# A gated linear recurrence and a token/channel mixer in one kernel: fp32 prefix sums in batch 0, upper halves read in place, and a written-out order

## The chip, the cores and the metric

The kernel runs on one core of one Trainium2 chip. The metric is the device time of one execution in microseconds, smaller is better. PE is the tensor engine, DVE the vector engine, ACT the scalar engine, POOL the GpSimd engine, SP the engine whose queue issues most transfers.

## The reference

All inputs are fp32. Per batch (4) and head (8) a state of 48 x 48 is decayed and updated over 768 steps; its output, laid out as 768 x 384 per batch, goes through a mixer.

```python
f = 1.0 / (1.0 + np.exp(-f_logit))
for t in range(S):
    state = f[:, :, t, :, None] * state + np.einsum('bhd,bhe->bhde', k[:, :, t], v[:, :, t])
    y[:, :, t] = np.einsum('bhd,bhde->bhe', q[:, :, t], state)
x = y.transpose(0, 2, 1, 3).reshape(B, S, H * D)
h = np.maximum(x.transpose(0, 2, 1) @ w_tok1, 0.0) @ w_tok2      # 768 -> 256 -> 768
u = x + h.transpose(0, 2, 1)
out = u + np.maximum(u @ w_ch1, 0.0) @ w_ch2                     # 384 -> 1536 -> 384
```

## The kernel before

The recurrence is done in chunks. A group (b,d) is batch b and one third d of the sequence, 256 steps on 128 partitions, two steps in each. For a group the kernel does this, by the names of its operations:

- four loads of 384 KB on SP's queue (`ldf`, `ldq`, `ldk`, `ldv`, L412), each into one of a few tiles per input;
- `exp` and `ln` on ACT (L536, L538) turn f_logit into Ln = log(1 + exp(-f)), the negative log of the gate; `P` on DVE (L543) adds the two steps of a partition into Pf;
- `hi` (ACT or POOL) casts Pf to bf16 in Phi, `lo` (L548) puts the rest Pf - Phi in Plo; `cums` on PE multiplies both with a triangular matrix (L556, L557: the prefix sums) and with two column masks (L561, L562: the totals), so that bf16 matmuls give nearly fp32 sums;
- `S0` on DVE (L566) subtracts Ln from the sums, which gives those of the even step; `gl`, `G`, `Gi` on ACT (L574, L577, L579) are the exponentials of the totals, of the negative sums and of the sums;
- `qh`, `kh` (L607, L618) are q and k times these factors, in bf16; they are transposed, on PE in batches 0 and 1 (L641) and by a transposing transfer in batches 2 and 3 (L653); `ev` copies them out of PSUM;
- `sc` on PE (L769, L725) are scores, `mk` on DVE (L776, L733) masks them into AmT, `av` (L786, L740) multiplies with v in bf16 (`U`, v_bf); `ds` (L672, L662) is the state's increment, `s`, `t`, `M`, `bm`, `bs` carry the state, `qm`, `qn` (L798, L749) add its share to y; `xev` (L823) copies y to xu, and `xb` casts it to x_bf.

After the three groups of a batch comes its mixer: `tok1` (L839), Relu `h1` (L844), `tok2` (L855), the add `u` (L861), a cast to u_bf, transposes `uP` (L876) and their copy `uT`, then `ch1` (L902) with Relu `z` on ACT or DVE (L909, L911), `ch2` (L927), the add `o` (L937) and the stores (L946), two per pair of row tiles, all on SP's queue.

w_tok1 and w_tok2 are loaded as fp32 by SP after batch 0's loads and cast on chip; w_ch1 and w_ch2 are loaded by POOL's queue, which converts them to bf16, in two halves each, behind a copy (`gate_`, L435) that waits for an earlier load.

No engine's order is written by hand. Each operation is given to a `Planner` with the engines that may do it, a cost for each, its inputs and outputs, and a priority `prio`, by default a due time from `due`, `at` and `at_gate`. `Planner.run` (L87) walks through planned time: of all ready operations it takes the one that can start first, and among equals the one with the smallest `prio`. It also chooses the tile from each pool and the PSUM bank (8 banks; `P.spare` keeps bank 7 out of use until planned time 26). The program is then issued in planned order, and each engine works through its queue strictly in that order, whatever the real times are. Where PE's plan has a gap before planned time 60, matmuls on a constant tile `idle` (L983, called fillers here) are put in, so that PE doesn't stand still.

Of the kernel before, what the change touches and what calls it, by code (L numbers as in the profile page):

```python
# [8 lines left out]
FP32 = mybir.dt.float32  # L9
# [3 lines left out]

SEM = 0.06
PE_LAT = 0.10
SW_LEAD, HW_LEAD = 3.9, 3.7


def act_t(n):
    return (0.05 + 0.835e-3 * n, 0.12)  # L20

# [8 lines left out]

def pe_mode(name):

    if name.startswith("sc"):
        return "s"
    if name.startswith("ds"):
        return "d"
    return "v" if name.startswith("av0") else "n"
# [7 lines left out]
class Planner:  # L45


    def __init__(self):
        self.ops, self.by_name = [], {}
        self.pools, self.group_pool, self.group_of = {}, {}, {}  # L50
        self.producers, self.touch = {}, {}
        self.bank_pools, self.banks, self.quota, self.warm = {}, [], None, 0.0
        self.held, self.spare, self.slack, self.patience = [], 0.0, {}, 0.0
# [33 lines left out]
    def run(self):  # L87
# [31 lines left out]
        while ready:  # L119
            best = None  # L120
            cache = {size: self._banks(size) for size in (1, 2)}
            for o in ready:
# [23 lines left out]
                for e, (occ, lat) in o.eng.items():  # L146
# [6 lines left out]
                    key = (round(st + self.patience * max(o.prio, -20.0), 2), o.prio, st + occ)  # L153
# [17 lines left out]
            if o.xfer is not None and e == "POOL":  # L171
# [12 lines left out]
                end = sw + 0.3  # L184
# [49 lines left out]
    @staticmethod  # L234
    def switch(a, b):
        if a == b:
            return 0.0
        return (0.095 if a == "s" else 0.0) + (0.093 if b != "n" and a != "s" else 0.0)
# [22 lines left out]
def kernel(  # L261
# [23 lines left out]
    XB_FROM = 2  # L285
    DEEP = 2
# [28 lines left out]
    Pf_tiles = [st([128, H, D], FP32, f"Pf{i}") for i in range(2)]  # L315
    P.pool("Pf", Pf_tiles)
    L_tiles = [(st([128, H, 64], BF16, f"Phi{i}"), st([128, H, 64], BF16, f"Plo{i}")) for i in range(2)]
    P.pool("L", L_tiles)
    P.pool("U", [st([128, 2, DM], BF16, f"v_bf{i}") for i in range(3)])
# [27 lines left out]
    P.patience = 0.0  # L347
    P.spare = 26.0
# [29 lines left out]
    def consts():  # L378
# [4 lines left out]
        for hi, lo in L_tiles:  # L383
            nc.vector.memset(hi[:, :, D:64], 0.0)
            nc.vector.memset(lo[:, :, D:64], 0.0)
        nc.vector.memset(halves, 0.0)
# [6 lines left out]
        nc.vector.tensor_scalar(tri2[0:64, 0:64], tri[0:64, 0:64], -1.0, None, ALU.add)  # L393
        for r in (slice(0, 64), slice(64, 128)):
# [13 lines left out]
    def load(nm, b, d, prio, after=()):  # L408
# [4 lines left out]
             prio, after, xfer=ROW * 128 * H)  # L413

    for b in range(B):
        seq = [(nm, c + 1 if nm == "f" else c) for c in range(-1, NP) for nm in "fqkv"]
        if b == 0:
            seq = [(w[0], int(w[1])) for w in "f0 f1 q0 k0 f2 v0 q1 k1 v1 q2 k2 v2".split()]
# [8 lines left out]
    gates = dict(zip(("wc1a", "wc1b", "wc2a", "wc2b"), ("w2s1", "-", "q1,1", "-")))  # L427
    sw = []

    def sw_dma(nm, outs, fn, n, mb):  # L430
# [6 lines left out]
        P.op(nm, {"POOL": (0.7 * n, 0)}, [], outs, fn, -899.5 + len(sw), dep, xfer=mb / 0.31)  # L437
        sw.append(nm)
    w1s = st([128, 3, 2, DT], FP32, "w1s")

    def flat(v):
        return P[v].rearrange("p h two d -> p (h two d)")
    tail = f"~ldv0,{NP - 1}"
    for n in range(2):
        P.value(f"w2s{n}", f"w2s{n}", "vk"[n])
    P.op("w1l", {"SP": (0.7, 0)}, [], ["w1s"], lambda: nc.sync.dma_start(
        out=w1s.rearrange("p g two c -> p g (two c)"),
        in_=moe_w_tok1.rearrange("(g p two) c -> p g (two c)", p=128, two=2)), -400, [tail], xfer=0.786 / 0.35)
    tail = "~w1l"
    for j in range(2):  # L450
        for kk in range(2):
            P.op(f"w1c{j},{kk}", {"POOL": pool_t(768), "ACT": act_t(768)}, ["w1s"], [f"w1{kk}"],
                 lambda e, j=j, kk=kk: cast(
                     e, w_tok1[64 * j:64 * j + 64].rearrange("p (g kk) c -> p kk g c", kk=2)[:, kk],
                     w1s[64 * kk:64 * kk + 64, :, j]), T0 - LEAD - 4 + kk)
    for kt in range(2):
        P.op(f"w2l{kt}", {"SP": (0.7, 0)}, [], [f"w2s{kt}"],
             lambda kt=kt: nc.sync.dma_start(out=flat(f"w2s{kt}"), in_=moe_w_tok2[128 * kt:128 * kt + 128]),
             -390 + kt, [tail], xfer=0.393 / 0.35)
        tail = f"~w2l{kt}"  # L460
        for th in range(2):
            P.op(f"w2{kt},{th}", {"ACT": act_t(384), "DVE": dve_t(384)}, [f"w2s{kt}"], [f"w2{th}"],
                 lambda e, kt=kt, th=th: cast(
                     e, w_tok2[:, kt, 384 * th:384 * th + 384].rearrange("r (c two p) -> r c two p", two=2, p=64),
                     flat(f"w2s{kt}")[:, 384 * th:384 * th + 384].rearrange(
                         "r (c p two) -> r c two p", p=64, two=2)), T0 - LEAD - 2 + th)
    P.by_name["ldf1,0"].after = (tail,)
    for hf in range(2):
        cols = slice(hf * (DCH // 2), (hf + 1) * (DCH // 2))
        sw_dma("wc1" + "ab"[hf], ["wc1" + "ab"[hf]], lambda cols=cols: nc.gpsimd.dma_start(  # L470
            out=w_ch1[:, :, cols], in_=moe_w_ch1.rearrange("(kt p) n -> p kt n", p=128)[:, :, cols]), 1, 1.18)
    for hf in range(2):
        kts = slice(hf * (NCC // 2), (hf + 1) * (NCC // 2))
        sw_dma("wc2" + "ab"[hf], ["wc2" + "ab"[hf]], lambda kts=kts: nc.gpsimd.dma_start(
            out=w_ch2[:, kts], in_=moe_w_ch2.rearrange("(kt p) n -> p kt n", p=128)[:, kts]), 1, 1.18)

    def cast(e, o, x):
        if e == "ACT":
            nc.scalar.copy(o, x)  # L479
        else:  # L480
            (nc.vector if e == "DVE" else nc.gpsimd).tensor_copy(o, x)  # L481
# [11 lines left out]
    def attention(b, d):  # L493
# [21 lines left out]
        P.value(f"Ln{i}", f"fld{i}", "f")  # L515
# [15 lines left out]
        def qkT(z, e):  # L531
# [3 lines left out]
        P.op(f"exp{i}", {"ACT": act_t(768)}, [f"f{i}"], [f"E{i}"],  # L535
             lambda: nc.scalar.activation(f_(), f_(), AF.Exp, bias=0.0, scale=-1.0), pg - 6)  # L536
        P.op(f"ln{i}", {"ACT": act_t(768)}, [f"E{i}"], [f"Ln{i}"],
             lambda: nc.scalar.activation(f_(), f_(), AF.Ln, bias=1.0, scale=1.0), pg - 5.5)  # L538
        flex = {"POOL": pool_t(384, True), "DVE": dve_t(384)} if b == 0 else {"POOL": pool_t(384, True)}

        def vec(e):
            return nc.vector if e == "DVE" else nc.gpsimd
        P.op(f"P{i}", {"DVE": dve_t(384)}, [f"Ln{i}"], [f"Pf{i}"], lambda: nc.vector.tensor_tensor(  # L543
            P[f"Pf{i}"][:, :, 0:D], f_()[:, :, 0], f_()[:, :, 1], ALU.add), pg - 5, port=True)
        P.op(f"hi{i}", {"POOL": pool_t(384), "ACT": act_t(384)}, [f"Pf{i}"], [f"hi{i}"],
             lambda e: cast(e, P[f"L{i}"][0][:, :, 0:D], P[f"Pf{i}"][:, :, 0:D]), pg - 4.5)
        P.op(f"lo{i}", flex, [f"hi{i}", f"Pf{i}"], [f"L{i}"],
             lambda e: vec(e).tensor_tensor(  # L548
                 P[f"L{i}"][1][:, :, 0:D], P[f"Pf{i}"][:, :, 0:D], P[f"L{i}"][0][:, :, 0:D], ALU.subtract), pg - 4,
             port=True)  # L550

        def cums():
            o = P[f"S1{i}"][:, 1]
            hi, lo = P[f"L{i}"]
# [9 lines left out]
        P.op(f"cums{i}", {"PE": (0.54, PE_LAT)}, [f"L{i}", f"hi{i}"], [f"S1{i}"], cums, pg - 3.5 + pe,  # L564
             after=[] if g2 < 0 or gi_sb else [f"~av{b2},1", f"~ds{b2}"])
        P.op(f"S0{i}", {"DVE": dve_t(384)}, [f"S1{i}", f"Ln{i}"], [f"S{i}"], lambda: nc.vector.tensor_tensor(  # L566
# [5 lines left out]
        def gi_out():  # L572
            return f_().rearrange("t h j d -> t j h d") if gi_sb else sv()
        P.op(f"gl{i}", {"ACT": (0.12, 0.12)}, [f"S1{i}"], [f"gl{i}"], lambda: nc.scalar.activation(  # L574
# [6 lines left out]
            after=[f"G{i}", f"gl{i}"] + ([f"S0{i}", f"P{i}"] if gi_sb else []))  # L581
# [12 lines left out]
        else:  # L594
            P.op(f"U{i}", {"POOL": pool_t(768), "ACT": act_t(768)} if b == 0 else {"POOL": pool_t(768)}, [f"v{i}"],
# [34 lines left out]
        if not xbar:  # L630
            for j in range(2):
                T = f"T{i},{j}"
                for nm in "qk":
# [8 lines left out]
                    P.op(f"tr{nm}{i},{j}", {"PE": (0.25, PE_LAT)}, [f"{nm}h{i},{j}"], [f"{T}{nm}"], tr,  # L642
# [7 lines left out]
        else:  # L650
            for e in range(2):
# [3 lines left out]
                         P[f"qh{i}"][64 * e:64 * e + 64]), pr - 500, xfer=1.3)  # L655
# [35 lines left out]
        if whole:  # L691
            P.op(f"bs{i}", {"ACT": (0.55, 0.12), "POOL": (0.6, 0.1)}, [f"s{i}"], [f"bs{i}"], lambda e: bs(e), pr + 2.05)
        else:
            P.op(f"bs{i}", {"ACT": (0.55, 0.12)}, [f"dS{i}"], [f"bs{i}"], bs, pr + 1.5, excl=f"dS{i}")
# [326 lines left out]
```

## Time and profile before

| | us |
|---|---|
| median of 4 runs (lowest, highest) | 184.63 (184.15, 185.4) |
| profiled execution, own time | 184.15 |
| its span, first to last instruction | 182.4 |
| PE, DVE, ACT, POOL busy | 169.6, 121.2, 119.3, 67.7 |
| first ch1 matmul / last ch2 matmul starts | 40.3 / 177.6 |

The span is from the first to the last instruction; the own time has about 1.75 us around it. Matmuls are pipelined: a row's duration of 326 ns for 384 columns is latency, and the next one starts about 162 ns later. The granted clock was 0.997.

### The profile page before, as it was taken

The numbers are of one execution on the slowest core, as the hardware profiler recorded it, in microseconds if no ns is written. First come the engines' busy times: TensorE is split into PE (matmuls) and PEld (weight loads), VectorE is DVE, ScalarE is ACT, GpSimd is POOL, SyncE is SP. The second block draws the span as 40 slices with busy tenths as digits, with TensorE's granted clock in tenths as the row PEclk, the third lists the DMA queues.
The fourth block names the chain that finished last, engine by engine and source line by source line (L and its number), as shares of the span: only waits on it lengthen the run. The fifth ranks groups of instructions, "written<-read, shape, count | busy, mean of one in ns | idle before, by whom it ended". The sixth has DMA issues, their size and how long they took to land.

```text
span 182.4 us, 5036 instructions
## 1 busy us (share of the span) xinstructions
PE 169.6 (93%) x2044; PEld 105.4 (58%) x2050; DVE 121.2 (66%) x232; ACT 119.3 (65%) x215; POOL 67.7 (37%) x114
## 2 busy tenths in 40 slices
PE   6999969999999999999989999789999999999990
PEld 2346646576566766565656666366666666666650
DVE  7479875698767687998499996998935166012021
ACT  2879689999676688767777935469238442924800
POOL 3017783466373347386543936265110100000000
PEclk9999999999999999999999999999999999999998
DMA  6999999999993999989999999991352021303033
GB/s 150 261 261 263 303 324 223 209 246 259 207 218 79 278 262 262 185 181 208 213 270 201 198 281 175 214 205 17 57 89 59 0 62 28 86 0 88 4 94 79
DMA packets 69159, 31.00 MB, mean 170 GB/s; under 512 B 63120, under 2 KB 68496, under 8 KB 69136
## 3 DMA queue, kind: packets, MB, share of 16 engines
q1 hardware_dynamic: 66768, 28.32, 73.2%
q0 software_dynamic: 2368, 2.36, 7.8%
q8 instruction: 16, 0.26, 0.6%
q14 instruction: 7, 0.06, 0.1%
HBM read 25.17 MB, written 4.72 MB: 164 GB/s over the span
## 4 chain that ended last, share of the span: by engine, by line
PE 63%; DVE 13%; ACT 11%; DMA 6%; issue 3%; DVEq 0%; POOL 0%; ACTq 0%; POOLq 0%
PE pp L902 24%; PE pp L927 22%; DMA v_ld<-in_v_dram 4%; DVE xu L861 3%; DVE qkh L618 3%; PE pp L855 3%; ACT f_ld L538 2%; ACT f_ld L536 2%; DMA f_ld<-in_f_logit_dram 2%; PE pp L839 2%; PE pp L725 2%; ACT xu L823 2%; PE pp L876 1%; PE pp L740 1%; DVE qkh L607 1%
## 5 line engine op out<-in xcount | busy, mean ns | idle before, releaser
L927 PE MATMUL pp<-w_ch,zT 128*128 128x384 bf16 x288 | 52.2, 326 | 0.0
L902 PE MATMUL pp<-uT,w_ch 128*128 128x384 bf16 x288 | 51.5, 326 | 0.6 <-DVE zT L911 0.4
L909 ACT ACTIVATE zT<-pp 128x384 bf16<-128x384 f32 x72 | 34.9, 490 | 18.1 <-PE pp L902 17.9
L902 PEld LDWEIGHTS <-w_ch 128*128 128x128 bf16 x288 | 26.9, 98 | 17.2 <-issue 1.0
L927 PEld LDWEIGHTS <-zT 128*128 128x128 bf16 x288 | 27.0, 98 | 16.5 <-issue 0.2
L937 DVE TENSOR_TENSOR xu<-xu,pp 128x384 f32<-128x384 f32 x24 | 13.2, 551 | 29.2 <-PE pp L927 29.0
L481 POOL CAST v_bf<-v_ld 64x384 bf16<-64x384 f32 (+1 forms) x28 | 16.1, 576 | 16.2 <-DMA v_ld<-in_v_dram 12.7
L983 PE MATMUL pp<-idle 128*128 128x512 bf16 (+5 forms) x76 | 19.7, 346 | 1.7 <-DVE idle L379 1.5
L776 DVE TENSOR_TENSOR AmT<-pp,msk 128x1024 bf16<-128x1024 f32 x12 | 14.4, 1219 | 3.1 <-PE pp L769 3.1
L911 DVE TENSOR_SCALAR zT<-pp 128x384 bf16<-128x384 f32 x24 | 12.7, 554 | 4.6 <-PE pp L902 3.7
L733 DVE TENSOR_TENSOR AmT<-pp,msk 128x1024 bf16<-128x1024 f32 x12 | 14.1, 1217 | 2.4 <-PE pp L725 2.3
L481 POOL CAST x_bf<-xu 128x768 bf16<-128x768 f32 x10 | 8.2, 822 | 20.0 <-ACT xu L823 20.0
L607 POOL TENSOR_TENSOR qkh<-q_ld,G 128x384 bf16<-128x384 f32 x14 | 13.0, 940 | 2.4 <-ACT glast L574 2.3
L618 DVE TENSOR_TENSOR qkh<-k_ld,pp 64x384 bf16<-64x384 f32 x24 | 13.2, 550 | 0.5
L983 PEld LDWEIGHTS <-idle 128*128 128x128 bf16 x82 | 8.0, 106 | 8.6 <-issue 3.6
L861 DVE TENSOR_TENSOR xu<-xu,pp 128x384 f32<-128x384 f32 x24 | 11.7, 546 | 0.2 <-PE pp L855 0.2
L536 ACT ACTIVATE f_ld<-f_ld 128x768 f32<-128x768 f32 x12 | 10.1, 839 | 2.6 <-DMA f_ld<-in_f_logit_dram 2.5
L548 POOL TENSOR_TENSOR Plo<-Pf,Phi 128x384 bf16<-128x384 f32 x10 | 9.1, 912 | 7.1 <-ACT Phi L479 3.2
L823 ACT COPY xu<-pp 128x768 f32<-128x768 f32 x11 | 8.8, 797 | 4.4 <-PE pp L786 2.3
L577 ACT ACTIVATE G<-pp 128x768 bf16<-128x768 f32 x12 | 9.7, 812 | 2.7 <-DVE pp L566 2.6
L855 PE MATMUL pp<-h1T,w_tok 128*128 128x384 bf16 x48 | 9.9, 325 | 1.0 <-DVE xu L937 0.6
L479 ACT CAST u_bf<-xu 128x768 bf16<-128x768 f32 x8 | 6.5, 831 | 6.4 <-DVE xu L861 6.2
(99 smaller groups left out, 246.7 us busy)
## 6 DMA issues: line engine op xcount, KB each, us to landing
f_ld<-in_f_logit_dram SPq DMA_DIRECT2D x12, 384.0 KB, 5.0
q_ld<-in_q_dram SPq DMA_DIRECT2D x12, 384.0 KB, 6.0
k_ld<-in_k_dram SPq DMA_DIRECT2D x12, 384.0 KB, 5.9
v_ld<-in_v_dram SPq DMA_DIRECT2D x12, 384.0 KB, 6.4
out_dram<-xu SPq DMA_DIRECT2D x22, 192.0 KB, 2.8
w_ch<-in_moe_w_ch_dram POOLq DMA_DIRECT2D x4, 576.0 KB, 9.3
w1s<-in_moe_w_tok_dram SPq DMA_DIRECT2D x1, 768.0 KB, 7.6
v_ld<-in_moe_w_tok_dram SPq DMA_DIRECT2D x1, 384.0 KB, 6.1
```

The lines of the kernel that those rows point to most:

```text
L481: (nc.vector if e == "DVE" else nc.gpsimd).tensor_copy(o, x)
L536: lambda: nc.scalar.activation(f_(), f_(), AF.Exp, bias=0.0, scale=-1.0), pg - 6)
L607: vec(e).tensor_tensor(o, x, g, ALU.mult)
L618: nc.vector.tensor_tensor(o, x, g, ALU.mult)
L733: lambda e=e: nc.vector.tensor_tensor(P[f"Am{e}{i}"], P[f"A{e}{i}"].rearrange("p b (a t) -> p (b a) t", t=128), msk2.rearrange("p j t -> p ...
L776: lambda j=j: nc.vector.tensor_tensor(P[f"Am{j}{i}"], P[f"A{j}{i}"].rearrange("p b (a t) -> p (b a) t", t=128), msk[:, j].rearrange("p j t ...
L855: nc.tensor.matmul(pm[:, 0:DM], lhsT=w_tok2[:, kt, tt * 128:(tt + 1) * 128], rhs=P[f"h1{b}"][:, kt, :], start=(kt == 0), stop=(kt == 1))
L861: nc.vector.tensor_tensor(x, x, P[f"up{i}"][:, 0:DM], ALU.add)
L902: nc.tensor.matmul(pm, lhsT=w_ch1[:, kt, cc * 128:(cc + 1) * 128], rhs=uT[:, 3 * th:3 * th + 3, kt, :], start=(kt == 0), stop=(kt == 2))
L909: nc.scalar.activation(P[f"z{i}"], P[f"zp{i}"][:, 0:384], AF.Relu)
L927: nc.tensor.matmul(P[f"op{i}"][:, 0:DM], lhsT=P[f"z{b},{th},{cc}"][:, c0:c0 + 128], rhs=w_ch2[:, cc, :], start=(cc == 0), stop=(cc == NCC ...
L983: nc.tensor.matmul(P.psum_tile[:, bank, 0:n], lhsT=idle[:, 0:128], rhs=idle[:, 0:n], start=True, stop=True)
```

## The change

1. `HIV`: the upper half of Pf is no longer cast into Phi. `hi_of` views the fp32 tile Pf as bf16 and takes every second element, so it is cut off, not rounded; `lo` is Pf minus that view. This holds in every group that still uses bf16 sums.
2. `F32P`: in batch 0, groups (0,1) and (0,2), the sums are fp32 matmuls on Pf itself: `mln` (minus Ln by a negative identity), `cums` (both halves of S at once) and `cumt` (the totals). `lo` and `S0` fall away there.
3. The order: `RANKS`, a table of 967 numbers, replaces the priority of every operation. Costs in the planner are changed a little, and bank 7 is kept out of use until planned time 30.
4. The last row tile of batch 3: ch2 and its add are done in two halves of 192 columns, and the stores of the last two tiles go to two queues, SP's and ACT's.
5. Loading and casting of w_tok1 and w_tok2 stay (`WSW = 0`, `COLS = 0`); the code for another way is not used.

The changed kernel's lines have other numbers: ch1 L1042, ch2 L1090 (last tile L1080), tok1 L973, tok2 L995, uP L1016, cums L650 and L651, fp32 sums L673, L679, L685, fillers L1153, stores L1109.

```diff
+RANKS = """
+560 561 562 563 564 565 566 567 568 569 570 571 573 574 575 576 577 578 579 580 581 582 583 584 587 588 589 590 591
...
+901 906 905 907 494 694 627 754 489 615 488
+"""
...
-                    key = (round(st + self.patience * max(o.prio, -20.0), 2), o.prio, st + occ)
+                    key = (int(st * 100.0 + 0.5), o.prio, st + occ)
...
+    HIV = 1
+    F32P = 2
+    F32 = 0
+    WSW = 0
...
-    Pf_tiles = [st([128, H, D], FP32, f"Pf{i}") for i in range(2)]
+    Pf_tiles = [st([128, H, 64 if HIV else D], FP32, f"Pf{i}") for i in range(2)]
...
-    P.spare = 26.0
+    P.spare = 30.0
...
+        f32p = F32P and b == 0 and d >= F32P - 1
...
+        def hi_of():
+            if HIV:
+                return P[f"Pf{i}"].bitcast(BF16).rearrange("p h (d two) -> p h d two", two=2)[:, :, :, 1]
+            return P[f"L{i}"][0]
...
+        def minus_ln():
+            nc.tensor.matmul(hd(P[f"S{i}"][:, 0, 0:DM]), lhsT=tri2f[:, 1], rhs=f_()[:, :, 1], start=True, stop=False,
+                             skip_group_check=True)
+
+        def cums32p():
+            x = P[f"Pf{i}"]
+            for a in (1, 0):
+                nc.tensor.matmul(hd(P[f"S{i}"][:, a, 0:DM]), lhsT=tri2f[:, 0], rhs=x[:, :, 0:D], start=(a == 1),
+                                 stop=(a == 0), skip_group_check=True)
+
+        def totals32p():
+            o, x = P[f"S{i}"][:, 1], blk(P[f"Pf{i}"])
+            for hp in range(HP):
+                nc.tensor.matmul(o[:, DM + 2 * hp:DM + 2 * hp + 2], lhsT=x[:, hp], rhs=halvesf, start=False,
+                                 stop=(hp == HP - 1), skip_group_check=True)
...
+            if b == B - 1 and tt == NCH - 1:
+                for n in range(2):
+                    c = slice(n * (DM // 2), (n + 1) * (DM // 2))
...
+                    def oadd(i=i, s=s, c=c, n=n):
+                        x = P[f"o{i}"][:, s, c]
+                        nc.vector.tensor_tensor(x, x, P[f"op{i},{n},0"][:, c], ALU.add)
...
+                if single:
+                    for j, (q_, e) in enumerate(((nc.sync, "SP"), (nc.scalar, "ACT"))):
+                        P.op(f"out{b},{tts[0]},{j}", {e: (0.6, 0)}, [f"o{b},{tts[0]}"], [],
+                             lambda store=store, j=j, q_=q_: store(js=(j,), eng=q_), due(b, "o", tts[-1]) - 500, xfer=0.45)
+                    continue
...
+    for o, rank in zip(P.ops, RANKS.split()):
+        o.prio = int(rank)
     total = P.run()
```

## The prediction

> **What bounds the kernel now.** I read the page's busy shares first, then the chain of waits, then the windows, then the groups by form.
>
> ```profile
> PE 169.6 (93%) x2044; PEld 105.4 (58%) x2050; DVE 121.2 (66%) x232; ACT 119.3 (65%) x215; POOL 67.7 (37%) x114
> ...
> DMA  6999999999993999989999999991352021303033
> ```
>
> PE looks full, but 82 of its matmuls are fillers (L983), and "busy" is pipelined time. So I price PE by start-to-start spacing. The chain of waits gives it: 36 matmuls of 384 columns in 5.85 us, 162.5 ns each; four 128-column transposes in 0.22; 32 scores in 0.57; 8 of L740 in 0.20; 4 of L749 in 0.17.
>
> ```profile
> 15.03 6.96 DMA v_ld<-in_v_dram
> 22.02 0.81 ACT v_bf L479
> ...
> 30.91 0.43 ACT w_tok L479
> 31.33 0.74 ACT f_ld L538
> 32.08 0.74 ACT xu L479 x2
> ...
> 35.77 2.66 DVE xu L861 x6
> ...
> 40.39 1.06 PE pp L902 x6
> ...
> 171.91 5.86 PE pp L927 x36
> 177.79 0.55 DVE xu L937
> ```
>
> Counting matmuls at these spacings, PE had 16.6 us of work before the first ch1 (L902, 40.3) and stood idle or on fillers for 23.7. From there to the last matmul (178.1) it had 128.2 us of work and lost 9.6: 1.9 in 40 to 60, 1.2 in 60 to 80, 2.1 in 80 to 112, **2.9 in 112 to 123** (batch 2's passage from tok1 to ch1), 1.5 after. So the time is the start, plus 128.2 of PE work, plus 9.6 of holes, plus a tail of 4.3. The start is no longer transfers alone: v of (0,2) lands at 22.0, but the last x_bf ends at 33.1, behind masks on DVE and weight casts on ACT.
>
> ```profile
> 20.00:30.00 10.00, 7.84 (x204) 5.66 (x206) 7.69 (x11) 7.50 (x11) 8.11 (x13) 1.00 1.05 304
> 30.00:40.00 10.00, 9.54 (x125) 6.44 (x125) 7.35 (x16) 9.94 (x18) 4.89 (x6) 1.00 1.08 216
> ```
>
> The columns that matter are the third and fourth engine, DVE and ACT: each has slack in the first stretch, and ACT none in the second.
>
> **What the Trainium skill says.** "FP8 and Floating Point Precision", TensorE Precision Notes: true FP32 is four passes through the array. No row of before shows it. Estimate from that page and our spacing: 4 x 160 ns = 0.64 us for 384 columns. "TensorE: Matmul & The Clock Gate", the section on 56 against 53.3 ns, gives N / 2.4 GHz + 2.5 ns and a floor of about 25 ns; the trace agrees (162.5 ns at 384, 25 ns for the 2-column L561). "SBUF — State Buffer", Door 1, says bf16 may be strided by up to 8 elements for free within 16-byte lines; the new upper halves step by 2, so they would cost nothing. No run here shows it yet.
>
> **The change part by part.**
>
> ```profile
> L479 ACT CAST Phi<-Pf 128x384 bf16<-128x384 f32 x8 | 4.1, 510 | 4.1 <-DVE Pf L543 4.0
> L481 POOL CAST Phi<-Pf 128x384 bf16<-128x384 f32 x4 | 2.3, 566 | 11.0 <-DVE Pf L543 11.0
> L548 POOL TENSOR_TENSOR Plo<-Pf,Phi 128x384 bf16<-128x384 f32 x10 | 9.1, 912 | 7.1 <-ACT Phi L479 3.2 <-issue 2.1 <-PE pp L855 1.5
> L556 PE MATMUL pp<-Phi,tri 128*128 128x384 bf16 x12 | 3.9, 325 | 0.0
> ```
>
> *Upper halves as a view.* All 12 Phi casts go: 4.1 us of ACT, 2.3 of POOL, and one hop per group. After batch 0 neither engine is the bound, so I cost that at nothing. In group (0,0) Plo follows Pf directly: 7.45 becomes 6.9, worth 0.5 at the first G. If strided reading ran at half speed, L556 and the four L561 would add 0.16 + 0.10 per group, 10 groups, 2.6 us; a gain in reading there cannot be. I take 0.
>
> *fp32 sums for (0,1), (0,2).* Out go a Plo (0.56 on DVE or 0.91 on POOL), an L566 (0.56 DVE) and a bf16 sum of about 0.53 on PE, twice. In come three fp32 matmuls of 384 (3 x 0.64 = 1.9) and four of 2 columns; for these I take 0.1 each (0.03 to 0.3), since four weight passes must be slower than one. That is 2.3 against 0.53 on PE, covered by fillers at 8 to 10.4. For (0,2) it is partly bare: score (0,1) and eight transposes of (0,1) stand behind it on PE; I put that score at 17.2, against 19.2 now. DVE loses 1.7 us and gains 0.45 of constants, which end before its first wait (6.3). Bounds for the start: -1 to +2.
>
> *Order table.* Every operation gets a rank; engines and tile slots are chosen again. I walked the new queues with the durations of the groups (back to back, DVE starts a 384-column operation every 0.47, masks every 1.12, ACT a 768-column one every 0.74). ACT without casts: exp and ln of (0,1) end at 7.9, G0 starts 9.0 (10.4 before), Gi0 ends 10.7. DVE: gates of (0,0) to 11.8, copies to 13.1 (both on DVE now), mask (0,0) 15.4, kh (0,1) to 17.5, mask (0,1) 17.8, masks of (0,2) from 24.6 to 26.9 instead of 28.2 to 30.5, one w_tok cast, the last x_bf at **28.5 instead of 33.1**. ACT keeps pace: w1s lands at 24.0, the w_tok2 halves at 25.0 and 26.3 as now, x copies at 27.4 to 28.3, f of (1,0) lands at 28.0. Then tok1 29.2, two Relus with an ln between 30.7, tok2, six adds and two Pf to 34.6, u_bf on POOL 35.0, transposes, uT 36.1: ch1 at **36.1 to 38; I take 37.0**, the upper part for waits that I do not see (the trace has 0.2 to 1.1 us of "issue" on PE). Queues passed: SP's first 15 loads keep their order; q and k of (0,2) now reuse the first tiles, free at 10.9 and 11.8, their issue 11.8 and 13.5, no wait. f of (1,1) must now wait on SP for kh (0,2) at 22 (it was issued at 20.5), with q, k and v of (1,0) behind it, but the transfers themselves are behind until 28. On POOL three w1s casts and an x_bf stand ahead of the w_ch1 issue: 27.7 instead of 27.07, landing 7.9 later as now, 35.6, and the second half 38.5 plus 0.7. So the weights nearly bind. The 16 transposes of (1,0) (0.9 us) move behind ch1. **Net of the start: -3.3 + 0.9 = -2.4** (-4 to +1).
>
> After that: (1) in 40 to 112 the holes were 5.2. ACT takes most Relus, no DVE pair of masks stands ahead of the first z; but batch 0's ch2 are used up before batch 1's passage, where six adds, four kh, a ch2 add and a state product precede one uT. DVE has 11 us there and PE 12, by the spacings above. I take 0 (-2 to +3). (2) Batch 2's passage: tok2 follows tok1 bare (Relu 0.5 + 0.2), then two adds less before the first two u_bf. Add 0.55, cast 0.83, transposes 0.33, copy 0.80 after the fourth tok2, less scores, transposes, sums in between: 1.9 of hole, was 2.9: **-1.0**. (3) Batch 3: all 18 transposes come together with one ch2 behind them, copy 0.80 less 0.49: **+0.5**.
>
> *Spare bank* until 30 instead of 26: holds a bank for fillers; I cost it inside the walk, since only planned order depends on it. *Weights*: same loads and casts, only other engines.
>
> *Tail.*
>
> ```profile
> 174.51 4.97 SPq L946 DMA_DIRECT2D out_dram<-xu  x6
> 175.91 0.56 DVE L937 TENSOR_TENSOR xu<-xu,pp 128x384 f32<-128x384 f32 x1 [1.47 <-PE pp L927]
> 177.79 0.55 DVE L937 TENSOR_TENSOR xu<-xu,pp 128x384 f32<-128x384 f32 x1 [1.33 <-PE pp L927]
> ```
>
> The last tile's 12 matmuls become 24 of 192 columns (82.5 ns by the page's formula, 24 x 82.5 = 1.98 against 1.95). The last add shrinks from 0.55 to 0.35 (192-column L697: 344 ns). Its two stores are issued at 178.3 and 178.9 on SP; now one each on SP and ACT, the second 0.5 earlier if ACT's issue is as quick, which no row shows (0 to 0.6 saved). **-0.6.**
>
> Sum: -2.4 - 1.0 + 0.5 - 0.6 = -3.5. From the profiled execution (span 182.4, own time 184.15, 1.75 around) 180.65; the median of four stands 0.48 above it: **181.1, say 181.0**.
>
> **Rivals.**
> *A, weights or unseen waits bind the start* (0.18). If w_ch1 lands some 2 us later, because more loads are queued ahead of it by then, ch1 starts at 39.3: start -0.1, total 183.3. For it: transfers are full to 40. Against: bytes and their order are the same.
> *B, the holes go too* (0.17). Relus move to ACT and ranks were set over all queues at once; if half of 9.6 goes beyond my sum, 181.0 - 3 = 178. Against: DVE keeps 12 + 12 masks at 1.2.
> *C, slower: the passage to ch1 runs bare in all three later batches* (0.18). PE has no ch2 left for filling there: add, cast, transposes, copy are 2.5 us; batch 1 +1.9, batch 2 +1.5 (two masks, 2.3 us, stand among the adds), batch 3 +2.0. Then +5.4 - 3.0 + 0.5 gives 187. It decides once the bare wait is over about 1.7 us per batch. For it: tok2 is followed at once by 18 transposes in batch 1. Against: DVE's own sum there is below PE's.
> *D, strided reading at half speed* (0.02): 2.6 us, 183.7, no change. That the view is not used can be excluded from the queues: no Phi cast is left.
>
> **Numbers.** The main case has 0.45 (179.3 to 183.0). Faster by over 0.5% (below 183.7; 0.5% is about what a measurement of this kernel tells from no change): main 0.45, B 0.17, 0.08 of A: 0.70. Same: 0.10 of A, D: 0.12. Slower: C, 0.18. Range 177.3 to 186.0: it leaves out the far end of B (0.05) and the upper part of C (0.12).
>
> **What would show it.** First ch1 near 37 with last x_bf near 28.5; fp32 matmuls 0.64 apart; L650 still 325 ns with 160 to its successor; PE's hole in batch 2's passage under 2; the last store issued within 0.5 of the last add. Wrong if ch1 starts after 39, if fp32 matmuls take over 1 us, or if PE waits over 1.7 us in each passage.

## The result, and the profile after

Median of the changed kernel: **186.03 us** (43 runs, 184.26 to 188.16); before, beside it, 184.81 us (64 runs). The ratio is 1.0038, 95% interval 1.002 to 1.0057: slightly slower, where 181.0 was forecast and 186.0 was the end of the range. The profiled execution took 184.55 us, its span is 182.8 us. These comparisons leave disturbed runs out.

The page after, busy shares and the clock by slices:

```profile
PE 170.2 (93%) x2046; PEld 107.6 (59%) x2051; DVE 117.5 (64%) x225; ACT 116.7 (64%) x209; POOL 64.9 (35%) x115
...
PEclk9999999999999999999999999999999999999999
```

As the diff says, DVE, ACT and POOL have less to do. But the first ch1 (now L1042) starts at 40.87, not at 37.0, and 0.9 us of transposes have moved behind it. The windows show where the holes went: the changed kernel first, then the one before; the third figure is TensorE's busy time.

```profile
80.00:84.00 4.00, 2.40 (x40) 1.85 (x39) 3.91 (x9) 2.70 (x4) 3.27 (x7) 1.00 0.90 167
...
116.00:124.00 8.00, 6.96 (x88) 4.01 (x87) 7.61 (x13) 4.79 (x9) 3.71 (x9) 1.00 0.99 173
```

```profile
80.00:84.00 4.00, 4.00 (x38) 2.41 (x37) 3.39 (x7) 2.77 (x5) 3.36 (x7) 1.00 1.07 259
...
116.00:124.00 8.00, 6.59 (x112) 4.25 (x112) 7.69 (x14) 4.85 (x9) 2.94 (x6) 1.00 1.09 211
```

Batch 1's passage (around 80) is worse, batch 2's (around 118) a little better. By the prediction's count (a hole is time of TensorE that its work, taken at start-to-start spacings, doesn't fill) the holes after the first ch1 fell by about 0.5 us: +1.5 to +1.9 in batch 1's passage, -0.8 to -0.9 in batch 2's, less than 0.2 either way after 124, and about -1.1 to -1.3 in the stretches between. The span's +0.4 is then the sum of a first ch1 that is 0.55 later, 0.4 more from there to the last matmul (0.9 of work more, 0.5 of holes less) and a tail that is 0.55 shorter.

What stands ahead of the first ch1 is seen best on TensorE's own timeline (start, duration, instruction, idle time before it), changed kernel:

```profile
25.45 0.23 PE L1153 MATMUL pp<-idle 128*128 128x128 bf16 x1
25.60 0.30 PE L903 MATMUL pp<-qkT 48*64 48x128 bf16 x5
27.47 0.36 PE L903 MATMUL pp<-qkT 48*64 48x128 bf16 x11 [1.57 <-issue]
```

A score of 16 matmuls stops behind its 5th for 1.57 us. "issue" says that nothing in the profile was waited for; all 16 read the same tile and write the same two banks by turns, and only the first of them waits for semaphores. The kernel before has the same thing, in another operation (L786 is the product with AmT):

```profile
25.94 0.29 PE L786 MATMUL pp<-v_bf,AmT 64*128 64x48 bf16 x9
27.30 0.25 PE L786 MATMUL pp<-v_bf,AmT 64*128 64x48 bf16 x7 [1.07 <-issue]
```

Counting all that the profile shows of TensorE (matmuls, weight loads and a few semaphore instructions) in order of start, the stop comes behind the 703rd instruction in the changed kernel and the 700th before. "Runtime: NRT & Kernel Launch", Instruction fetch mechanics, in the Trainium skill says that an engine's instructions come in blocks of 16 KiB, 256 instructions, by the engine's own DMA queue, the next block while the current one runs, "mostly hidden". The trace has such a queue, q8, with 16 packets of 16 KB beside TensorE's 4,097 matmuls and weight loads; one starts at 25.02 us, 2.45 us before TensorE goes on. That gave the main theory: **the stop is a late instruction block**, late because loads fill the DMA engines.

A second difference shows only over many runs. Each run has a mean granted clock. In the 22 runs of the changed kernel repeated below, the four at 1.0 took 184.32 us in the median; the twelve at 0.986 to 0.991 took 185.84. Of the kernel before, 22 of 52 beside them lay above 0.992, at 184.13, and 26 at 0.985 to 0.991, at 185.45. So the two kernels are 0.2 us apart at full clock and 0.4 at the lower one. About half of the shift of the median comes from these, the rest because the changed kernel is at full clock less often.

### The profile page after: what moved, and what is told of

The parts are those of the page before. It is cut to its first block, busy times and chain, and to the rows that moved or that the text cites. A ratio compares the mean times of both kernels' runs of the same rounds, so it can differ in the third digit from the quotient of the medians.

```text
span 182.8 us, 5027 instructions
## 1 busy us (share of the span) xinstructions
PE 170.2 (93%) x2046; PEld 107.6 (59%) x2051; DVE 117.5 (64%) x225; ACT 116.7 (64%) x209; POOL 64.9 (35%) x115
## 4 chain that ended last, share of the span: by engine, by line
PE 63%; DVE 13%; DMA 9%; ACT 4%; POOL 3%; issue 3%; SPq 2%; DVEq 0%; POOLq 0%; ACTq 0%
PE pp L1090 20%; PE pp L1042 19%; DMA q_ld<-in_q_dram 4%; DVE qkh L752 4%; PE pp L973 3%; PE pp L995 3%; DMA v_ld<-in_v_dram 2%; PE pp L775 2%; PE pp L1153 2%; DMA f_ld<-in_f_logit_dram 2%; SPq L787 2%; DVE xu L1001 2%; PE pp L920 2%; PE pp L903 2%; PE pp L932 2%
## 5 line engine op out<-in xcount | busy, mean ns | idle before, releaser
L1090 PE MATMUL pp<-w_ch,zT 128*128 128x384 bf16 x276 | 50.9, 326 | 0.3 <-DVE xu L1100 0.3
L1042 PE MATMUL pp<-uT,w_ch 128*128 128x384 bf16 x288 | 51.2, 326 | 0.0
L1049 ACT ACTIVATE zT<-pp 128x384 bf16<-128x384 f32 x81 | 39.1, 491 | 14.4 <-PE pp L1042 14.0
L1042 PEld LDWEIGHTS <-w_ch 128*128 128x128 bf16 x288 | 26.8, 98 | 16.8 <-DVE uT L499 0.2
L1090 PEld LDWEIGHTS <-zT 128*128 128x128 bf16 x276 | 25.7, 98 | 15.8 <-issue 0.4
L1153 PE MATMUL pp<-idle 128*128 128x512 bf16 (+7 forms) x58 | 15.5, 355 | 1.8 <-DVE idle L434 1.5
L642 POOL TENSOR_TENSOR Plo<-Pf 128x384 bf16<-128x384 f32 x9 | 7.4, 824 | 18.2 <-DVE Pf L631 16.1
L741 POOL TENSOR_TENSOR qkh<-q_ld,G 128x384 bf16<-128x384 f32 x13 | 11.7, 912 | 3.2 <-DMA q_ld<-in_q_dram 1.1
L622 ACT ACTIVATE f_ld<-f_ld 128x768 f32<-128x768 f32 x12 | 10.1, 841 | 2.5 <-DMA f_ld<-in_f_logit_dram 2.5
L995 PE MATMUL pp<-h1T,w_tok 128*128 128x384 bf16 x48 | 10.1, 325 | 0.5 <-ACT h1T L978 0.4
L1153 PEld LDWEIGHTS <-idle 128*128 128x128 bf16 x63 | 6.3, 108 | 7.1 <-issue 3.2
L624 ACT ACTIVATE f_ld<-f_ld 128x768 f32<-128x768 f32 x12 | 10.1, 842 | 0.2
```

The costliest lines, as they stand in the source:

```text
L741: vec(e).tensor_tensor(o, x, g, ALU.mult)
L995: nc.tensor.matmul(pm[:, 0:DM], lhsT=w_tok2[:, kt, tt * 128:(tt + 1) * 128], rhs=P[f"h1{b}"][:, kt, :], start=(kt == 0), stop=(kt == 1))
L1042: nc.tensor.matmul(pm, lhsT=w_ch1[:, kt, cc * 128:(cc + 1) * 128], rhs=uT[:, 3 * th:3 * th + 3, kt, :], start=(kt == 0), stop=(kt == 2))
L1049: nc.scalar.activation(P[f"z{i}"], P[f"zp{i}"][:, 0:384], AF.Relu)
L1090: nc.tensor.matmul(P[f"op{i}"][:, 0:DM], lhsT=P[f"z{b},{th},{cc}"][:, c0:c0 + 128], rhs=w_ch2[:, cc, :], start=(cc == 0), stop=(cc == NCC ...
L1153: nc.tensor.matmul(P.psum_tile[:, bank, 0:n], lhsT=idle[:, 0:128], rhs=idle[:, 0:n], start=True, stop=True)
```

## The experiments

"At full clock" is the median of a kernel's runs above 0.992; before stood at 184.51, 184.13, 184.25 and 184.49 in the four groups of runs.

**1. The end of batch 0: exchange two ranks.**

```diff
+    a, b = P.by_name["x00,2"], P.by_name["x10,2"]
+    a.prio, b.prio = b.prio, a.prio
```

> The changed kernel with the ranks of two operations exchanged, so that at the end of batch 0 the copy x00,2 (ACT) and the copy x10,2 come in the other order; nothing else is changed. Theory (the chain at the end of batch 0 sets the start): the second half of x_bf no longer waits for ACT's second copy, the last x_bf ends at about 32.2 instead of 33.1, the first channel product begins at about 39.9 instead of 40.87, and the time is 0.8 us less than the changed kernel's, at equal clock. Rival (what comes after it on ACT, the token products' Relu and the weights, is as late anyway): x_bf earlier, the first channel product still at 40.7 to 40.9, time within 0.2 us.

Timeline of the changed kernel, then of this one:

```profile
31.09 0.56 DVE L499 CAST x_bf<-pp 128x384 bf16<-128x384 f32 x1 [0.41 <-PE pp L920]
31.69 0.86 ACT L497 COPY xu<-pp 128x384 f32<-128x384 f32 x2 [2.99 <-DVE x_bf L499]
32.58 0.56 DVE L499 CAST x_bf<-pp 128x384 bf16<-128x384 f32 x1 [0.93 <-ACT xu L497]
```

```profile
30.81 1.11 ACT L497 COPY xu<-pp 128x384 f32<-128x384 f32 x2 [2.14 <-PE pp L920]
30.84 1.03 DVE L499 CAST x_bf<-pp 128x384 bf16<-128x384 f32 x2 [0.44 <-PE pp L920]
```

In the table's order DVE's and ACT's copies read the same half by turns, one behind the other; exchanged, the engines run side by side. x_bf ends 1.27 us earlier and the first ch1 starts at 39.84 instead of 40.87; 0.24 of that is a shorter stop (1.55 us from start to start instead of 1.79). For the start the theory held. The time is 183.82 at full clock instead of 184.3, where 0.8 less was expected (between the two profiles, both at a clock of 1.0, it is 1.0); the ratio to before is 0.9981 (0.9957 to 1.0005).

**2. Is the stop tied to a place in the program or to a count of instructions?** The 14 fillers of 64 columns left out:

```diff
-            if n < 64:
+            if n < 128:
```

> The changed kernel without those of TensorE's filler products that have 64 columns (fillers of 128 columns and more stay); only TensorE's queue is shorter, by about nine fillers ahead of the stop. Theory (TensorE stops at 25.9 because its next block of instructions has not come from memory): the stop of about 1.6 us stays, but at a place some 9 matmuls further on in the program, in the same score or behind it, because the boundary goes by the count of instructions. Rival (the stop is a wait for an operand or a bank that the trace does not show): it stays behind the 5th of the 16 matmuls of that score. Both expect the time within 0.5 us of the changed kernel.

```profile
25.54 0.41 PE L903 MATMUL pp<-qkT 48*64 48x128 bf16 x14
27.48 0.24 PE L903 MATMUL pp<-qkT 48*64 48x128 bf16 x2 [1.53 <-issue]
```

Same score, but now behind its 14th matmul instead of the 5th: nine further on, as expected, and again at the 703rd instruction. The count decides, so it is no wait for an operand or a bank. In all ten profiles that have the stop, of both kernels, it lies behind instruction 700 to 705 (some records can be missing). Time at full clock 184.12, ratio 1.002 (0.9994 to 1.0045).

**3. Table and fp32 sums, each taken out.**

```diff
-    for o, rank in zip(P.ops, RANKS.split()):
-        o.prio = int(rank)
```

> The changed kernel with the table of ranks left out: the order comes from the due times again, the other edits stay. If the table's order is what made the end of batch 0 late (serial copies, later masks), the first channel product is at 39.5 to 40.5 and the time is 0.5 us or more below the changed kernel's. If the table is what keeps batch 2's passage at 2.1 us of holes instead of 2.9, and the tail close, leaving it out costs 1 to 3 us, and the holes between 80 and 130 grow by that. Prediction's own sum: +1.5 us.

193.16 us, ratio 1.0442 (1.0396 to 1.0487): with the other edits in place the table is worth far more than the +1.5 given for it. (The kernel before has due times too and takes 184.8, so it is due times and the other edits together that cost this; which edit, no run shows.) The first ch1 starts at 40.89, so the start is no better without the table. Batch 2's passage is left bare, and part of it runs at half clock; this window against 14.96 busy in the changed kernel:

```profile
112.00:128.00 16.00, 11.14 (x139) 6.48 (x140) 11.94 (x23) 5.19 (x11) 6.80 (x13) 0.79 0.82 176
```

```diff
-    F32P = 2
+    F32P = 0
```

> The changed kernel with the fp32 sums of batch 0 taken back to the bf16 pair (upper half read in place, rest formed on POOL or DVE, S0 by DVE's subtraction); table and all else stay, each operation of the pair takes the place in the table of the one it stands for. Theory (the fp32 sums lengthen the start: 0.83 + 1.29 us and totals of 0.8 to 0.95 us on TensorE for each token tile, against 0.53 us): the first channel product is 0.3 to 0.8 us earlier than 40.87. Rival (TensorE has room there, and POOL's and DVE's operations that come back cost as much): 40.87 plus 0 to 0.6, time 0 to 0.6 us more.

First ch1 at 40.66 against 40.87, between the two cases expected. But this is no price of the sums in the start, because a second thing changed: though no load is held back here, the packet of the block starts at 22.59 instead of 25.02, and TensorE has no stop, neither at its 703rd instruction (25.50) nor in the scores, which run in one piece:

```profile
26.80 0.64 PE L903 MATMUL pp<-qkT 48*64 48x128 bf16 x32
```

With the stop gone from the changed kernel too (experiment 8), its first ch1 starts at 39.06, 1.6 us earlier than this one. The three runs at a clock of 1.0 took 187.5 to 188.9 us; the ratio is 1.0241 (1.0184 to 1.0297). Much of the loss lies in the passages: TensorE is busy for 10.89 us in 76 to 90 (12.40 in the changed kernel) and for 13.94 in 112 to 128 (14.96). The same ranks with other durations give other queues later, so this too is no clean price of the sums, and what exactly is late there was not followed up.

**4. Empty the DMA engines while the block is fetched.** The weights' and batch 1's loads wait on SP for a small write of DVE:

```diff
+    names = [x[2].name for x in P.order]
+    a, z = names.index("w1l"), names.index("ev0,2,0")
+    late = [x for x in P.order[a:z] if x[3] == "SP"]
+    P.order = [x for x in P.order[:a]] + [x for x in P.order[a:z + 1] if x[3] != "SP"] + late + P.order[z + 1:]
...
+            if o.name == "w1l":
+                nc.vector.memset(w1s[:, 0, 0, 0:1], 0.0)
```

> The changed kernel with the loads of the token weights and of batch 1 held back on SP's queue until DVE has done the copy of qkT that runs at 24.77 to 25.45 (a one-column write into w1s by DVE, which the load has to wait for); all else as it was, so the casts of the weights and batch 1 come some 7 us later. Theory (TensorE's stop at its 703rd instruction is a late fetch of its next 256 instructions, late because the 16 DMA engines are full of loads): with the engines nearly empty from about 22 us the fetch that now begins at 25.02 begins 2 us or more earlier, and the stop of 1.79 us at the 703rd instruction falls below 0.3 us. Rival (the fetch takes its 6 us whatever else the engines move): the stop stays, 1.3 us or more, at the 703rd instruction. Both expect a slower kernel as a whole, by 2 to 8 us, since the weights of the token products come late.

DMA view, 21.5 to 25.0 us: in the changed kernel the engines are full and q8 moves nothing; its packet comes in the stretch after, 25.0 to 27.5, shown second. In this kernel, third, the q8 packet (starting at 21.85) is one of the two that move at all from 21.5 to 25.0.

```profile
DMA packets 701, 1.37 MB, mean 391 GB/s; under 512 B 178, under 2 KB 178, under 8 KB 701
## 3 DMA queue, kind: packets, MB, share of 16 engines
q1 hardware_dynamic: 701, 1.37, 102.1%
```

```profile
DMA packets 1683, 0.70 MB, mean 282 GB/s; under 512 B 1664, under 2 KB 1664, under 8 KB 1681
## 3 DMA queue, kind: packets, MB, share of 16 engines
q1 hardware_dynamic: 1681, 0.68, 110.6%
q8 instruction: 1, 0.02, 2.7%
```

```profile
DMA packets 2, 0.02 MB, mean 7 GB/s; under 512 B 0, under 2 KB 0, under 8 KB 0
## 3 DMA queue, kind: packets, MB, share of 16 engines
q8 instruction: 1, 0.02, 1.7%
```

TensorE then does not stop; all 16 matmuls of the score run in one piece:

```profile
25.57 0.42 PE L903 MATMUL pp<-qkT 48*64 48x128 bf16 x16
25.92 0.50 PE L1159 MATMUL pp<-idle 128*128 128x512 bf16 x2
```

The stop is a fetch that loads delay, and all fifteen profiles agree with it. In the ten that have the stop the packet starts at 24.28 to 25.02, and TensorE goes on 2.4 to 2.6 us after that. In the five without it, the bf16 run of experiment 3 among them, the packet has started by 22.6, at least 2.9 us before TensorE is at its 703rd instruction. From the start of the instruction 256 places ahead of the stop (or of the 703rd) to the packet it takes 0.7 us here, 1.1 to 1.5 in the runs of experiments 7 and 8 that have no stop, 2.6 in the bf16 run and 3.2 to 4.3 in the ten. So "mostly hidden" does not describe this boundary: 1.79 us from start to start were not hidden in the changed kernel, 1.25 in the one before.

The kernel with the hold is slower as a whole (188.23, ratio 1.0177, 1.0125 to 1.023): token products wait for weights.

**5. The tail alone**, put into the kernel before (the last tile's halves and the store on ACT; the diff is that part of the change):

> The kernel before with one part of the change alone: the last tile's product in two column halves, each half added as it is done, and its two stores issued one on SP and one on ACT. Theory (the prediction's tail term): the stretch from the last matmul to the end of the span falls from 4.6 to 4.0 us, the time by 0.6 us at equal clock. Rival (the halves cost as much on TensorE as the shorter add saves): within 0.2 us.

183.71 at full clock against 184.13, ratio 0.9961 (0.9934 to 0.9988): -0.4 at full clock, a little under the term of -0.6.

**6. The clock.** The changed kernel again, and fillers in batch 1's passage on top of experiment 1:

```diff
+    s, bank = [(s, P.idle_bank(s - 1.2, s)) for s, _, o, e in P.order if o.name == "uP1,0"][0]
+    fillers["uP1,0"] = [(bank[1], 512)] * 5
```

> The changed kernel as it is, beside the others on one chip. Theory: runs at a mean clock of 1.0 take 184.3 to 184.6, runs at 0.985 to 0.991 take 1.5 us more, runs at 0.98 and below 3.2 us more, and only a quarter are at 1.0; in a profile with a mean clock below 1.0 the half clock begins within 3.5 us of the end of a stretch of 1 us or more in which TensorE did nothing (the stop at 25.7, the wait for x_bf at 32 to 35, the passage at 81), lasts 3.4 us and costs half of that where TensorE is what is waited for. Rival (the clock falls in stretches of dense work): the half clock begins behind 3.4 us or more of a full TensorE.

> The changed kernel with the two ranks exchanged (as in the kernel with the exchange alone) and with five filler products of 512 columns put into TensorE's queue in the passage from batch 1 to batch 2, ahead of the transposes of u that wait there for 1.57 us. Theory (a stretch without work on TensorE is followed by a window at half clock in part of the runs, and this stretch is one such place): TensorE is busy there, the time of a run at full clock stays that of the exchange alone (183.5 to 183.9), and runs at a mean clock below 0.992 become fewer than the 12 of 22 of the exchange alone. Rival (only the stop at the 703rd instruction brings on the half clock): the share of such runs stays at about half; and if the fillers get into the way, the time at full clock grows by up to 0.5 us.

The repeat's profile had a mean clock of 0.988. Windows of it; the clock is the third figure from the end:

```profile
23.00:25.80 2.80, 2.75 (x78) 2.21 (x69) 2.44 (x4) 2.38 (x3) 0.80 (x4) 1.00 1.03 383
25.80:29.20 3.40, 1.82 (x38) 0.87 (x32) 1.33 (x2) 2.86 (x7) 3.25 (x6) 1.00 0.97 235
29.20:32.60 3.40, 3.40 (x51) 2.26 (x50) 1.81 (x3) 0.00 (x0) 1.69 (x3) 0.50 1.05 232
32.60:36.00 3.40, 2.85 (x17) 1.46 (x16) 0.78 (x2) 2.72 (x5) 0.00 (x0) 1.00 1.15 207
```

The half clock follows a window with the stop in it, not a dense one; the theory held. "TensorE: Matmul & The Clock Gate" in the Trainium skill, Part 1: The HAM clock gate, says that activity is watched in free-running windows of 3,413 ns and that the clock is halved after an idle one. The trace agrees in the length (3.413 us); but here the window before was not idle, it was busy for 1.82 of its 3.4 us. The traces bear out a fixed grid within an execution, too: in the seven profiles that have two or more stretches at half clock, these start a whole number of windows apart (in the repeat at 29.20 and 182.80, 45 windows). In the first profile after, the same stop was there and the clock stayed. Its grid, counted back from the half clock that begins after the last instruction (183.88), has a border at 26.87, inside the stop, so that TensorE was busy for 2.40 and 2.65 us in the two windows that share it. Where the grid falls thus has a part in which runs are hit. It is not the busy time alone: in the profile of experiment 1 the clock stayed after a window that held the whole stop and was busy for 1.92, and in one of experiment 7 (the kernel before) it fell after one of 2.58. What else counts is open.

The added fillers run in the passage (1.24 us) and cost nothing: 183.72 at full clock, ratio 0.997 (0.9943 to 0.9996). That they make the half clock rarer is not shown: 10 of 22 runs below 0.992, 13 of 22 without them.

**7. Holds that keep the weights in time.** Same edit as in 4, with other bounds. First on top of exchange and fillers, from the second token weight on:

```diff
+    a, z = names.index("w2l0"), names.index("mk0,1,0")
...
+                nc.vector.memset(P["w2s0"][:, 0, 0, 0:1], 0.0)
```

> The changed kernel with the two ranks exchanged and the five fillers in batch 1's passage, and with the loads from the second token weight on (w2 in two halves, then batch 1) held on SP's queue until DVE has ended the mask that now runs at 21.14 to 22.37; only the first token weight stays ahead. Theory (the stop at the 703rd instruction is a fetch that is late behind loads): the fetch that begins at 25.0 begins at 24.0 or earlier, the stop of 1.25 to 1.8 us shrinks to below 0.5, the masks of token tile 2 end 1 us or more earlier, and as w2 lands at 26.5 to 28 the first channel product is at 38.8 to 39.3 (39.8 with the exchange alone): 182.7 to 183.2 at full clock, and the runs at half clock after the stop become rare. Rival (w2's casts on ACT come too late for the copies x and the token products): the first channel product at 39.8 or later, time as with the exchange or up to 1 us more.

The block is fetched at 22.32, there is no stop, and the last x_bf ends 2.8 us earlier than in the changed kernel:

```profile
25.55 0.42 PE L903 MATMUL pp<-qkT 48*64 48x128 bf16 x16
26.13 0.27 PE L1163 MATMUL pp<-idle 128*128 128x256 bf16 x1 [0.16 <-issue]
26.33 0.42 PE L903 MATMUL pp<-qkT 48*64 48x128 bf16 x16
```

```profile
29.26 1.03 DVE L499 CAST x_bf<-pp 128x384 bf16<-128x384 f32 x2 [0.42 <-PE pp L920]
```

First ch1 at 38.27. **181.50 us** (181.47 to 182.38, all six runs above 0.992), ratio to before 0.9803 (0.9763 to 0.9843): better than both kernels, and than the 182.7 to 183.2 expected.

Then with batch 1's loads alone held, and the same in the kernel before:

> As the one with w2 held, but only the loads of batch 1 are held, until DVE's copy of qkT at 24.77 to 25.45 is done; both token weights stay ahead. Theory: the weights' 1.5 MB keep the engines full until about 24, the fetch comes 0.3 to 1.0 us earlier than at 25.0, the stop shrinks by as much, the weights land earlier by 1 us; first channel product at 39.0 to 39.6, 183.0 to 183.6 at full clock. Rival (batch 1's loads then come late for batch 1): new holes between 40 and 60 give it back.

> The kernel before with the loads of batch 1 held on SP's queue until DVE has ended the product M of token tile 2 (23.4); nothing else is changed. Theory (its stop at the 700th instruction, 26.05 to 27.30, is the same late fetch): the fetch that begins at 24.79 comes up to 1 us earlier, the stop shrinks by as much, the first channel product is at 39.3 to 40.0 instead of 40.32, and the time is 0.3 to 1.0 us less, with fewer than half of the runs below a mean clock of 0.992. Rival: the stop stays as long, the time within 0.2 us, or it grows because batch 1 starts later.

With both weights still ahead of it the fetch comes at 24.38, a stop of 1.35 us (start to start) stays; 183.31 at full clock, ratio 0.9932 (0.9906 to 0.9958). Before: fetch at 24.28, 0.47 us of "issue" left of 1.07, 184.0 at full clock against 184.25, ratio 0.9953 (0.993 to 0.9976), mostly because 14 of 22 runs are now above 0.992 (14 of 43 unheld). Fetch and stop are as the theory has it. The forecasts of the first ch1 can't be judged: both profiles have a window at half clock ahead of it (it starts at 41.0 and 40.8).

**8. What the hold alone is worth, in each kernel.** The changed kernel with the hold of 7 only, and the kernel before with it (bound "t0,1"):

> The changed kernel with the hold of the loads from w2 on (until DVE has ended the mask at 21.14 to 22.37) and nothing else: no exchange of ranks, no added fillers. Theory (the late fetch of TensorE's instructions is what the prediction's start term missed most): the fetch begins at 22.3 as in the kernel with exchange, fillers and hold, no stop at the 703rd instruction, the last x_bf ends at about 31.2 (0.9 later than the 30.29 there, the serial copies remain), the first channel product at 39.2 instead of 40.87, the time 182.3 to 182.7 at full clock against 184.3, and nearly all runs at a mean clock above 0.992. Rival (the gain needs the exchange as well, because the copies x and x_bf wait for w2's casts on ACT): 183.5 to 184.3 at full clock.

> The kernel before with the loads from w2 on held on SP's queue until DVE has ended the addition to the state at 21.21 to 21.56; nothing else is changed. If the hold is worth the same in every order, the stop at the 700th instruction goes and the time falls by 1.5 to 2.5 us to 182 to 183. If the changed order is what makes room for it (in the kernel before, three of w2's casts stand on DVE ahead of the masks of token tile 2, so a later w2 delays the masks), the stop goes but the masks start no earlier than 28.0, the first channel product stays at 40.0 to 40.6, and the time falls by 0.2 to 0.8 us, mostly through fewer runs at half clock.

The masks of (0,2), which wait for the scores; the changed kernel, then with the hold:

```profile
27.87 2.35 DVE L910 TENSOR_TENSOR AmT<-pp,msk 128x1024 bf16<-128x1024 f32 x2 [2.42 <-PE pp L903]
```

```profile
26.08 2.35 DVE L910 TENSOR_TENSOR AmT<-pp,msk 128x1024 bf16<-128x1024 f32 x2 [0.62 <-PE pp L903]
```

Changed: no stop, the masks start 1.79 us earlier, which is the length of the stop, first ch1 at 39.06, 182.35 at full clock, ratio 0.9874 (0.983 to 0.9918): the stop was worth 1.8 us of start and 2.0 of time. Before: first ch1 at 39.38, 183.45 at full clock, ratio 0.9927 (0.9903 to 0.995); the masks start at 26.95, so neither of the two cases expected: half the gain. With the fetch in time in both, the change itself is worth about 1.1 us.

The held changed kernel also shows the second place where the clock falls, batch 1's passage:

```profile
78.50 0.50 PE L1016 MATMUL pp<-ident,u_bf 128*128 128x128 bf16 x6
80.34 0.86 PE L1016 MATMUL pp<-ident,u_bf 128*128 128x128 bf16 x12 [1.35 <-POOL u_bf L499]
```

```profile
78.50:81.90 3.40, 1.80 (x36) 1.51 (x35) 3.32 (x8) 2.40 (x3) 2.74 (x6) 1.00 0.95 170
81.90:85.30 3.40, 3.40 (x12) 1.58 (x13) 1.05 (x3) 1.41 (x3) 1.31 (x4) 0.50 1.05 269
```

## Why the prediction was wrong

**The start, forecast -2.4, measured about +1.45** (first ch1 0.55 later, 0.9 of transposes behind it). This is the term that failed: "ch1 at 36.1 to 38; I take 37.0". The 3.9 us to 40.87 come apart by the runs:
- *1.8: the late instruction block.* The new order packs TensorE's queue: the 256 instructions ahead of the stop took 4.4 us (5.2 before), while the next block was there only some 6.2 after the first of them began. The walk named 0.2 to 1.1 us of "issue" as waits it did not see and gave them room in a range; the 1.1 was this stop, in view, and it was not asked what it was. It grew from 1.07 to 1.57 because TensorE came there 0.37 us sooner (25.68 against 26.05) and went on 0.17 later.
- *0.8 to 1.0: the copies at the end.* "x copies at 27.4 to 28.3" beside the last x_bf at 28.5: the walk let DVE and ACT run side by side where their order makes each wait for the other.
- *1.3: the rest*, still there with both gone (38.27 against 37.0). The masks of (0,2) start at 26.02 against 24.6 in the walk. Its q lands at 19.2, 7.4 us after its issue, against 6.3 before. Why it takes longer was not tried.

**The median over the profiled run**, taken as +0.48, was 1.5: the half clock comes more often, and costs 1.5 a time.

**The end of the matmuls.** The last matmul of the kernel before ends at 177.76 in its trace; the prediction's 178.1, and 177.6 as its start, are too late. The holes it counted were thus some 9.3 us and the tail 4.6, with the same sum.

**fp32 sums.** 0.65 to 0.68 us for 384 columns, as estimated (0.64). Groups by form after:

```profile
L679 PE MATMUL pp<-Pf,tri2f x8: 486/486/569, 8.6 to 16.5; 128*128 128x384 f32 x8
...
L685 PE MATMUL pp<-halvesf,Pf x16: 167/251/252, 9.9 to 17.5; 128*128 128x2 f32 x16
```

The profile shows two instructions for each fp32 matmul. The 2-column totals took 0.8 to 0.95 us for four, 0.2 each, not 0.1. Score (0,1) started at 17.76 against 17.2.

**The strided upper half** cost nothing, as taken: L650 lasts 335 ns (L556: 325) and its successor starts 0.17 later. Rival D (half speed) is out.

**The passages.** Batch 2's: 2.1 us of holes against 1.9 forecast and 2.9 before; right. Batch 1's: forecast 0 with -2 to +3, measured +1.5 to +1.9. Batch 3's +0.5 did not come: after 124 the holes are the same within 0.2. Rival B (half of the holes go too) is out, since they fell by 0.5 in all. Rival C (bare in all three) came true in batch 1 alone as a loss; its point, 1.7 us of waits, was passed in batches 1 and 2, but batch 2's was passed before as well.

**The tail** was right in the profile: 4.05 us from the last matmul to the end, 4.6 before. Lines after:

```profile
176.58 2.14 PE L1070 MATMUL pp<-w_ch,zT 128*128 128x192 bf16 x24
...
177.44 2.21 ACTq L1109 DMA_DIRECT2D out_dram<-xu  x2
177.77 0.35 DVE L1080 TENSOR_TENSOR xu<-xu,pp 128x192 f32<-128x192 f32 x1 [0.37 <-PE pp L1070]
178.76 0.35 DVE L1080 TENSOR_TENSOR xu<-xu,pp 128x192 f32<-128x192 f32 x1 [0.64 <-PE pp L1070]
```

Rival A (weights or unseen waits bind the start) came nearest in size of the start, and of its two causes the unseen wait was the right one. The weights did not bind: in experiment 7 the first ch1 starts 2.6 us earlier although w2's loads are issued 3.3 us later, and the first half of w_ch1 lands at 36.8, 1.5 us ahead of it.

## What to carry to other kernels

An "issue" stop in the middle of a run of like matmuls is to be counted in instructions and set beside the instruction queue's packets: where TensorE takes 256 small instructions in less time than a fetch behind full DMA engines needs (here 4.4 us against 6.2), packing its queue tighter only lengthens the stop. Hold back loads that are not needed yet. And stops of over a microsecond on TensorE cost twice, once themselves and, in part of the runs, a window at half clock (here 1.5 us of time); compare medians only beside the mean clock of the runs.

## What was not expected of the hardware

- The next 256 instructions of TensorE came 6.2 us after the block before was begun (from the instruction 256 ahead of the stop to the restart, 21.25 to 27.47, in the changed kernel) with the DMA engines full; with them nearly empty the fetch began 3.2 us earlier (21.85) and no stop was left.
- A half-clock window came after windows of 3.4 us in which TensorE was busy for 1.82 and 1.80 (the two profiles above); a full idle window was not needed. Yet the clock also stayed once after 1.92, so a stop of this size does not always bring it on.
- An fp32 matmul of 2 columns took 0.2 us here (L685), eight times the 25 ns of the bf16 one (L655).
